# Streamed weight sums and x in the free halves of the weight slots, w_out left where it is, and new byte addresses for g

## The chip, the core and the metric

The kernel runs on one NeuronCore of a Trainium2 chip. The metric is the device time of one execution, in microseconds. The core's engines take their instructions in order, each from its own queue, and meet at semaphores: TensorE (PE; its weight loads are listed as PEld), VectorE (DVE), ScalarE (ACT), GpSimd (POOL), and SyncE (SP), which here issues every DMA.

## The reference, cut to what matters

```python
def _attn_ref(q, k, v):                      # [8, 8, 576, 64], in chunks of 64 rows
    scores = scale * np.matmul(q_c, k_c.transpose(0, 1, 2, 4, 3))
    scores = scores - np.max(scores, axis=-1, keepdims=True)
    attn = np.exp(scores)
    attn = attn / (np.sum(attn, axis=-1, keepdims=True) + 1e-09)
    return np.matmul(attn, v_c)
def _moe_ref(x, w_in, w_out):                # x [4608, 512] is the attention's output
    h = x @ w_in                             # w_in [512, 2048]
    g = h * (1.0 / (1.0 + np.exp(-1.702 * h)))
    return (g @ w_out).astype(np.float32)    # w_out [2048, 512]
```

w_in and w_out come as float64, the rest as float32.

## The kernel before, in words

**Numbers as two words.** Every large product takes its operands as a high and a low float32r word, and one product is three matmuls: high times low, high times high, low times high (L1018 to L1020 and L624 to L626 for h, L1054 to L1056 for the second product, called o below).

**Tiles and batches.** The 4608 tokens are 36 tiles of 128, in 9 batches n of 4 tiles (512 tokens). The 2048 hidden units are 16 blocks j of 128, and g = 16 n + j counts blocks over the whole run. For each block PE makes h in one PSUM bank (`hp`, two buffers), ACT applies the gate and writes `g_h`, DVE writes `g_l`, and PE adds the block's share to four accumulating banks `po` (one for each token tile, 12 matmuls of 512 columns for a block, stationary side `g_h` or `g_l`, moving side the words of w_out). After 16 blocks ACT or DVE copies `po` to `ob` (two buffers) and a DMA stores it.

**Batches 0 and 1** make h directly: 12 matmuls of 512 columns for each block, stationary the words of w_in, moving x. **Batches 2 to 8** make h for two blocks at a time (a pair p, 8 of them) by a seven-product scheme for 2 x 2 blocks: 7 products of 6 matmuls of 256 columns in four phases (`phase`, L624 to L626), whose results DVE and ACT put together (L629, L634). Its stationary operands are three blocks of w_in as they are and four sums of blocks; its moving operands are seven forms of x.

**Slots.** Sixteen slots `w0` to `w15` of 8 KB in each partition hold a block's weights after they are read and split: the first half of a slot, `wt[j][:, 0]`, the words of w_in, the second half, `wt[j][:, 1]`, those of w_out. Before its weights arrive a slot serves the attention of the first tiles.

**The preparation** (`plan_prep`, for each pair) runs while batches 0 and 1 compute. POOL forms the sums (L505 to L515), ACT and DVE split them into words in a tile of their own, `split` (L525 to L533, in slot 0 or 1 by turns from pair 1 on), and DMAs write it all to a scratch tensor `seven` in DRAM: the three plain blocks (`out_a`, L538) and the sums (`out_s`, L548). The words of w_out are written to a second scratch tensor, `second` (`out_o`, L542), and read back pair by pair into slots 8 to 15 (`in_o`, L553), because slots 1 to 6 turn into x of the even batches (`xo`) and into the ring.

**The ring.** In batches 2 to 8 the operands of every pair are read from `seven` again, in four loads (L614; 256 KB, then three of 512 KB) into a ring of six places of 4 KB for each partition: two in each of slots 5 and 6, one in slot 4, one in the second half of `xe3`. A place is free once its phase has run. x of the odd batches lies in `xe0` to `xe3`.

**The attention** of token tiles u and u + 1 (a pair of tiles) runs between the blocks: DMAs bring q and k rows (`raw`, L733 and L722, 32 or 64 small DMAs), DVE transposes them (L776), PE makes the scores s of this pair and x of the pair before in one step (L792, L866), then DVE, ACT and POOL make the softmax and DVE transposes it (L841). From batch 2 on ACT stages x in `xa` and `xb` (L900), POOL forms differences (L470) and ACT and DVE write the words (L473, L476).

**What sets the order.** All steps are given to `Plan` with an engine, a cost, a rank and the events that they need; `Plan.emit` plays them through on its own clock, and the order that comes out is the order in each engine's queue. The first steps follow a list, `ORDER`. A DMA's cost there is the time that it holds SP's queue, plus a fixed `HANDOVER`. `LEAD` is how many blocks ahead of its pair a ring load gets its rank.

**Addresses.** Tiles lie one behind the other in each partition. `gelu`, a tile of 32 bytes that only serves to load a table, stands in the middle of them. Slots 0, 1, 3 and 8 to 15 and `xe0` to `xe3` lie ahead of it and start at 128 modulo 512 bytes. Slots 2, 4, 5, 6 and 7 (so the ring), and `g_h` and `g_l` lie behind it and start at 160 modulo 512. All offsets within these tiles that a matmul uses are multiples of 512 bytes.

## Time and profile before

| | |
|---|---|
| median of 3 runs | 868.02 us (866.17 to 869.13) |
| the profiled execution | 871.12 us, span of the core 869.3 us |
| PE busy / weight loads busy | 839.4 us (97%) / 732.8 us |
| DVE / ACT / POOL busy | 550.1 / 380.6 / 123.2 us |
| DMA traffic | 189.91 MB; mean 218 GB/s |
| granted clock of TensorE, mean | 0.99 |

A span runs from the first to the last instruction. Matmuls are pipelined, and their listed durations overlap (one of 512 columns is listed with about 0.40 us though the next starts 0.23 us later); what a matmul costs is read from one start to the next. A row of the timeline gives start, duration, engine, source line, operation, the tiles written and read, shapes and, in brackets, how long the engine had been idle and which instruction ended that. Batch 0 runs to about 136 us, batch 1 from 130 to 243 us, and batches 2 to 8 from 229 us to the end.

### The profile page before, as it was taken

The numbers are of one execution on the slowest core, as the hardware profiler recorded it, in microseconds if no ns is written. First come the engines' busy times: TensorE is split into PE (matmuls) and PEld (weight loads), VectorE is DVE, ScalarE is ACT, GpSimd is POOL, SyncE is SP. The second block draws the span as 40 slices with busy tenths as digits, with TensorE's granted clock in tenths as the row PEclk, the third lists the DMA queues.
The fourth block names the chain that finished last, engine by engine and source line by source line (L and its number), as shares of the span: only waits on it lengthen the run. The fifth ranks groups of instructions, "written<-read, shape, count | busy, mean of one in ns | idle before, by whom it ended". The sixth has DMA issues, their size and how long they took to land.

```text
span 869.3 us, 17292 instructions
## 1 busy us (share of the span) xinstructions
PE 839.4 (97%) x6902; PEld 732.8 (84%) x6902; DVE 550.1 (63%) x788; ACT 380.6 (44%) x556; POOL 123.2 (14%) x102
## 2 busy tenths in 40 slices
PE   7999989799899988999999999999999999999998
PEld 6788877688788877888988888988888989889886
DVE  5788865562665757675867586758675866634333
ACT  5999725352435234344534353435343534423222
POOL 1000163930300020002100020003000300200000
PEclk9999989899999999999999999999999999999999
DMA  9996877995796779888877788888966676557551
GB/s 228 327 292 185 255 223 213 358 344 140 237 281 210 203 215 265 233 228 202 229 211 210 202 213 248 202 209 233 261 173 178 183 222 180 169 170 219 174 165 49
DMA packets 241216, 189.91 MB, mean 218 GB/s; under 512 B 187248, under 2 KB 201584, under 8 KB 239216
## 3 DMA queue, kind: packets, MB, share of 16 engines
q1 hardware_dynamic: 241136, 188.80, 76.6%
q8 instruction: 55, 0.90, 0.4%
q14 instruction: 25, 0.20, 0.1%
HBM read 156.24 MB, written 32.51 MB: 217 GB/s over the span
## 4 chain that ended last, share of the span: by engine, by line
PE 78%; DMA 11%; SPq 7%; ACT 2%; DVE 1%; issue 1%; DVEq 0%; ACTq 0%
PE po L1054 13%; PE po L1056 13%; PE po L1055 13%; PE hp L625 9%; PE hp L626 9%; PE hp L624 9%; DMA ring<-seven 4%; SPq L733 3%; PE hp L1018 3%; PE hp L1020 2%; PE hp L1019 2%; DMA out_dram<-ob 2%; PE s L792 2%; PE x L866 1%; SPq L297 1%
## 5 line engine op out<-in xcount | busy, mean ns | idle before, releaser
L1054 PE MATMUL po<-second,g_l 128*128 128x512 f32 x448 | 179.1, 400 | 2.3 <-DVE ob L1065 1.8
L1055 PE MATMUL po<-second,g_h 128*128 128x512 f32 x448 | 177.0, 395 | 0.0
L1056 PE MATMUL po<-second,g_h 128*128 128x512 f32 x448 | 176.9, 395 | 0.0
L629 DVE TENSOR_TENSOR d<-hp,d 128x512 f32<-128x512 f32 x168 | 85.5, 509 | 134.1 <-PE hp L626 131.4
L656 ACT ACTIVATE d<-d 128x512 f32<-128x512 f32 x56 | 35.4, 632 | 289.5 <-DVE d L629 289.4
L1056 PEld LDWEIGHTS po<-second,g_h 128*128 128x128 f32 x448 | 84.2, 188 | 20.4
L1054 PEld LDWEIGHTS po<-second,g_l 128*128 128x128 f32 x448 | 84.3, 188 | 18.3 <-DVE ob L1065 2.4
L1055 PEld LDWEIGHTS po<-second,g_h 128*128 128x128 f32 x448 | 84.3, 188 | 14.3
L624 PE MATMUL hp<-xo,ring 128*128 128x256 f32 x320 | 90.1, 281 | 2.6 <-DVE g_l L1045 1.7
L625 PE MATMUL hp<-xo,ring 128*128 128x256 f32 x320 | 90.2, 282 | 0.0
L626 PE MATMUL hp<-xo,ring 128*128 128x256 f32 x320 | 90.1, 281 | 0.0
L822 POOL TENSOR_TENSOR e<-e,r 128x1024 f32<-128x1024 f32 x16 | 32.8, 2051 | 392.8 <-DVE r L819 362.0
L841 DVE STREAM_TRANSPOSE eT<-e 32x512 f32<-32x512 f32 x120 | 84.2, 702 | 5.6 <-POOL e L822 3.8
L624 PE MATMUL hp<-xe,ring 128*128 128x256 f32 x272 | 76.4, 281 | 2.2 <-issue 2.2
L626 PE MATMUL hp<-xe,ring 128*128 128x256 f32 x272 | 76.5, 281 | 0.0
L625 PE MATMUL hp<-xe,ring 128*128 128x256 f32 x272 | 76.5, 281 | 0.0
L661 DVE TENSOR_TENSOR g_l<-f,g_h 128x512 fp32r<-128x512 f32 x56 | 44.7, 799 | 35.5 <-ACT g_h L657 35.4
L624 PEld LDWEIGHTS hp<-xo,ring 128*128 128x128 f32 x320 | 60.4, 189 | 6.4 <-DVE g_l L1045 1.9
L625 PEld LDWEIGHTS hp<-xo,ring 128*128 128x128 f32 x320 | 60.4, 189 | 3.0
L626 PEld LDWEIGHTS hp<-xo,ring 128*128 128x128 f32 x320 | 60.6, 189 | 0.0
L624 PEld LDWEIGHTS hp<-xe,ring 128*128 128x128 f32 x272 | 51.2, 188 | 5.0 <-issue 2.8
L1054 PE MATMUL po<-w,g_l 128*128 128x512 f32 x128 | 52.2, 408 | 2.4 <-ACT ob L1063 2.0
(145 smaller groups left out, 1709.3 us busy)
## 6 DMA issues: line engine op xcount, KB each, us to landing
ring<-seven SPq DMA_DIRECT2D x131, 512.0 KB, 4.5
xe<-seven SPq DMA_DIRECT2D x37, 512.0 KB, 4.5
ring<-seven SPq DMA_DIRECT2D x56, 256.0 KB, 3.2
raw<-in_moe_w_in_dram SPq DMA_DIRECT2D x16, 512.0 KB, 7.6
raw<-in_moe_w_out_dram SPq DMA_DIRECT2D x16, 512.0 KB, 7.6
second<-w SPq DMA_DIRECT2D x16, 512.0 KB, 5.2
out_dram<-ob SPq DMA_DIRECT2D x32, 256.0 KB, 3.2
second<-second SPq DMA_DIRECT2D x8, 1024.0 KB, 8.1
```

The costliest lines, as they stand in the source:

```text
L624: nc.tensor.matmul(hp[:, o], w[:, 0, c], xl[:, c], start=c == 0, stop=False)
L625: nc.tensor.matmul(hp[:, o], w[:, 0, c], xh[:, c], start=False, stop=False)
L626: nc.tensor.matmul(hp[:, o], w[:, 1, c], xh[:, c], start=False, stop=c == 1)
L629: add = lambda out, a, b: nc.vector.tensor_tensor(out, a, b, op=ALU.add)
L656: nc.scalar.activation(t, t, AF.Gelu_apprx_sigmoid)
L661: nc.vector.tensor_tensor(gl, words(h), gh.bitcast(F32), op=ALU.subtract)
L733: nc.sync.dma_start(t[p0 : p0 + 32, i, n, o // 32 : (o + c) // 32, :], src[b, 2 * n + h, s : s + c, d * 32 : d * 32 + 32].rearrange("(t j) ...
L822: nc.gpsimd.tensor_tensor(st["e"], st["e"], bc(st["r"]), op=ALU.mult)
L841: nc.vector.transpose(st["et"][po : po + 32, :, 32 * a : 32 * a + 32], st["e"][pi : pi + 32, :, 32 * b : 32 * b + 32],)
L1054: nc.tensor.matmul(po, gl[:, c], w[:, 0, :], start=j == 0, stop=False)
L1055: nc.tensor.matmul(po, gh[:, c], w[:, 0, :], start=False, stop=False)
L1056: nc.tensor.matmul(po, gh[:, c], w[:, 1, :], start=False, stop=j == NF - 1)
```

## The change

The words of w_out stay in the second halves of their slots for the whole run; `second`, `out_o` and `in_o` are gone. Two exceptions are moved once, by a DMA within SBUF: those of slot 0 to the first half of slot 1 and those of slot 7 to the first half of slot 2, because slots 0 and 7 are used as whole tiles later (`xb`, `raw`). The first halves take what had slots of its own: x of the even batches in slots 3, 4, 5, 6, 8, 9 and 10, and the ring in slots 11 to 15; the sixth place stays in `xe3`. The sums of a pair are split into the first halves of the pair's own two slots, over the words of w_in, so a pair's split needs both h of batch 1 on that pair and the three plain blocks written out; then two DMAs of 512 KB write it to `seven`. Ring places are handed out first come, first served. `Plan` gets a fourth resource, `bus`: a bulk DMA holds SP for 0.5 us and then one shared bus for its cost. `LEAD` goes from 8 to 12 and `EARLY` (the rank of the attention steps) from 4 to 3. `gelu` is 512 bytes instead of 32, which puts all slots, `g_h` and `g_l` at 128 modulo 512.

```diff
+
+    def bulk(self, cost, rank, fn, need=(), make=None, take=(), give=()):
+
+        self.add(DMA, 0.5, rank, fn, need=need, make=make + "~", take=take)
+        self.add(BUS, cost, rank, None, need=[make + "~"], make=make, give=give)
...
-    EARLY = 4
+    EARLY = 3
     K_ACT = (1, 2, 3, 4)
-    LEAD = 8
-    PREP = 4
-    PREP_FROM = 15
+    LEAD = 12
...
     seven = dram.tile([NF // 2, P, 7 * 512], F32, tag="seven", name="seven")
-    second = dram.tile([NF // 2, P, 2 * 1024], F32, tag="second", name="second")
-    X_SLOT, MIXED, RING, SECOND_RAW, W_OUT = (1, 2, 3), 4, (5, 6), 7, 8
     PLAIN = 2
+    STAGE, SECOND_RAW = 0, 7
+    MOVED = {STAGE: 1, SECOND_RAW: 2}
+    X_SLOT, RING = (3, 4, 5, 6, 8, 9, 10), (11, 12, 13, 14, 15)
...
     def x_part_of(n, i, hl):
 
-        if i < 6:
-            return held["x", n % 2, i // 2][:, hl, i % 2]
-        return held["x", n % 2, 3][:, 0, hl]
+        if n % 2:
+            return held["x", i // 2][:, hl, i % 2] if i < 6 else held["x", 3][:, 0, hl]
+        return wt[X_SLOT[2 * (i // 2) + hl]][:, 0, i % 2] if i < 6 else wt[X_SLOT[6]][:, 0, hl]
 
     def x_tile(k):
-        held["x", 1, k] = const.tile([P, 2, 2, 512], F32R, tag=f"xe{k}", name=f"xe{k}")
-        if k == 3:
-            held["r", NRING - 1] = held["x", 1, 3][:, 1].rearrange("p w f -> p (w f)")
+        held["x", k] = const.tile([P, 2, 2, 512], F32R, tag=f"xe{k}", name=f"xe{k}")
...
         for i, k, hneed in ((0, 2, st_a), (2, 2, [e("t1")]), (4, 2, [e("t2")]), (6, 1, [e("t4")])):
             if n == PLAIN:
-                hneed = hneed + [f"al_{X_SLOT[i // 2] if i < 6 else MIXED}"]
+                hneed = hneed + [f"po_{X_SLOT[min(i + 1, 6)] // 2}"]
             if n == PLAIN + 1:
                 hneed = hneed + [f"xal_{i // 2}"]
             plan.add(ACT, 0.55 * k, rank, lambda i=i, k=k: hi(i, k), need=hneed, make=e(f"h{i}"))
...
-        tags = ("stage", "wtmp") if p == 0 else (f"w{(p - 1) % 2}",)
-
-        def hi():
...
+        def half(i):
+            return wt[2 * p + i][:, 0].rearrange("p a b -> p (a b)").rearrange("p (s w f) -> p s w f", s=2, w=2)
+
+        def hi(i):
+            nc.scalar.activation(half(i)[:, :, 0], st["s"][:, 2 * i : 2 * i + 2], AF.Copy)
+
+        def lo(i):
+            w = half(i)
+            nc.vector.tensor_tensor(
+                w[:, :, 1], st["s"][:, 2 * i : 2 * i + 2], w[:, :, 0].bitcast(F32), op=ALU.subtract
+            )
 
-        def out_o(u):
-            w = wt[2 * p + u][:, 1].rearrange("p w f -> p (w f)").bitcast(F32)
-            nc.sync.dma_start(second[p, :, 1024 * u : 1024 * u + 1024], w)
...
-        def in_o():
-            held["o", p] = t = const.tile([P, 2, 2, 512], F32R, tag=f"w{W_OUT + p}", name=f"second_{p}")
-            nc.sync.dma_start(t.rearrange("p u w f -> p (u w f)").bitcast(F32), second[p])
-
-        rank, late = PREP + 2 * p, 11 + p
+        def out_s(i):
+            at = 1024 + 1024 * i
+            w = wt[2 * p + i][:, 0].rearrange("p a b -> p (a b)").bitcast(F32)
+            nc.sync.dma_start(seven[p, :, at : at + 1024], w)
+
+        first = (PLAIN - 1) * NF + 2 * p
+        rank = first - 2
         e = lambda a: f"{a}_{p}"
         w0, w1 = f"w_{j0}", f"w_{j1}"
-        plan.add(POOL, 1.05, rank, lambda: whole(0), need=[w0, f"w_{PREP_FROM}"], make=e("pa0"), take=["tmp"])
+        outs = [e(f"pout{i}") for i in range(3)]
+        for i in range(3):
+            plan.bulk(0.75, first - 6, lambda i=i: out_a(i), need=[w0 if i < 2 else w1], make=outs[i])
+        plan.add(POOL, 1.05, rank, lambda: whole(0), need=[w0, f"w_{NF - 1}"], make=e("pa0"), take=["tmp"])
         plan.add(POOL, 1.05, rank, lambda: whole(1), need=[w1, e("pa0")], make=e("pa"))
         plan.add(POOL, 2.4, rank, sums, need=[e("pa")], make=e("psum"), take=["tmp"], give=["tmp"])
-        plan.add(ACT, 1.08, rank, hi, need=[e("psum")], make=e("phi"), take=[("tmp" if t == "wtmp" else t) for t in tags])
-        plan.add(DVE, 1.25, rank, lo, need=[e("phi")], make=e("plo"), give=["tmp"])
-        outs = []
-        for i in range(3):
-            outs.append(e(f"pout{i}"))
-            plan.add(DMA, 0.6, late, lambda i=i: out_a(i), need=[w0 if i < 2 else w1], make=outs[-1])
         for i in range(2):
-            outs.append(e(f"oout{i}"))
-            plan.add(DMA, 0.6, late, lambda i=i: out_o(i), need=[w0, w1][i : i + 1], make=outs[-1])
-        outs.append(e("pouts"))
-        plan.add(DMA, 1.4, rank, out_s, need=[e("plo")], make=e("pouts"), give=[("tmp" if t == "wtmp" else t) for t in tags])
-        plan.add(None, 0, rank, None, need=outs, make=e("po"))
-        plan.add(DMA, 1.4, PLAIN * NF + 2 * p - 4, in_o, need=[e("po")], make=e("second"), take=[f"w{W_OUT + p}"])
+            plan.add(
+                ACT, 0.6, rank, lambda i=i: hi(i), need=[e("psum"), f"h_{first + 1}", e("pa")] + outs, make=e(f"phi{i}"),
+            )
+            plan.add(
+                DVE, 0.69, rank, lambda i=i: lo(i), need=[e(f"phi{i}")] + [e("plo0")] * i, make=e(f"plo{i}"),
+                give=["tmp"] * i,
+            )
+            plan.bulk(1.44, rank, lambda i=i: out_s(i), need=[e(f"plo{i}")], make=e(f"pouts{i}"))
+        plan.add(None, 0, rank, None, need=[e("pouts0"), e("pouts1")], make=e("po"))
...
     def plan_slots():
-        def ring(k):
-            t = const.tile([P, 2, 1024], F32R, tag=f"w{(MIXED, *RING)[k]}", name=f"ring_{k}")
-            if k:
-                held["r", 2 * k - 1] = t[:, 0]
-            else:
-                held["x", 0, 3] = t[:, :1].rearrange("p o (w f) -> p o w f", w=2)
-            held["r", 2 * k] = t[:, 1]
-
...
-        for j in range(NF):
-            done = [f"o_{(PLAIN - 1) * NF + j}_{t}" for t in range(TB)] + [f"po_{j // 2}"]
-            plan.add(None, 0, -1000, None, need=done, give=[f"w{j}"])
-            if j in X_SLOT:
-                plan.add(None, 0, -1000, lambda j=j: odd(j - 1), need=done + ["prepped"], make=f"al_{j}", take=[f"w{j}"])
-            elif MIXED <= j < SECOND_RAW:
-                plan.add(None, 0, -1000, lambda j=j: ring(j - MIXED), need=done, make=f"al_{j}", take=[f"w{j}"])
+        def move(a, b):
+            nc.sync.dma_start(wt[b][:, 0].bitcast(F32), wt[a][:, 1].bitcast(F32))
+
+        for a, b in MOVED.items():
+            g = (PLAIN - 1) * NF + a
+            plan.bulk(1.44, g, lambda a=a, b=b: move(a, b), need=[f"po_{b // 2}"], make=f"moved_{a}")
+            done = [f"o_{g}_{t}" for t in range(TB)] + [f"po_{a // 2}", f"moved_{a}"]
+            plan.add(None, 0, -1000, None, need=done, give=[f"w{a}"])
         for k in range(4):
             need = [f"h_{(PLAIN - (k < 2)) * NF - 1}"]
             plan.add(None, 0, -1000, lambda k=k: x_tile(k), need=need, make=f"xal_{k}")
-        plan.add(None, 0, -1000, None, need=[f"po_{p}" for p in range(NF // 2)], make="prepped")
+        flat = lambda t: t.rearrange("p a b -> p (a b)")
+        for j in RING:
+            plan.add(None, 0, -1000, lambda j=j: ring_free.append(flat(wt[j][:, 0])), need=[f"po_{j // 2}"], give=["ring"])
+        plan.add(None, 0, -1000, lambda: ring_free.append(flat(held["x", 3][:, 1])), need=["xal_3"], give=["ring"])
...
     def plan_seven(n, p):
         g0 = n * NF + 2 * p
-        first = ((n - PLAIN) * (NF // 2) + p) * 4
         st = {}
         e = lambda a: f"{a}_{g0}"
-        slot = lambda i: held["r", (first + i) % NRING]
-
         def load(i):
             a, b = LOADS[i]
-            nc.sync.dma_start(slot(i)[:, : 512 * (b - a)].bitcast(F32), seven[p, :, 512 * a : 512 * b])
+            st["w", i] = ring_free.pop(0)
+            nc.sync.dma_start(st["w", i][:, : 512 * (b - a)].bitcast(F32), seven[p, :, 512 * a : 512 * b])
...
         for i, (a, b) in enumerate(LOADS):
-            q = first + i
-            need = [f"al_{MIXED + (q + 1) // 2}"] if q < NRING - 1 else ["xal_3"] if q < NRING else [phase_of[q - NRING]]
-            phase_of[q] = e(f"ph{i}")
+            plan.bulk(
+                0.72 * (b - a), g0 - LEAD + 0.1 * i, lambda i=i: load(i), need=[f"po_{p}"], make=e(f"ld{i}"), take=["ring"],
+            )
             plan.add(
-                DMA, 0.5 * (b - a), g0 - LEAD, lambda i=i: load(i), need=need + [f"po_{p}"], make=e(f"ld{i}"),
+                None, 0, g0, lambda i=i: ring_free.append(st["w", i]), need=[e(f"ph{i}")], give=["ring"],
             )
...
         def o_pe(t):
             gh, gl = g_t[g]
-            w = held["o", j // 2][:, j % 2] if n >= PLAIN else wt[j][:, 1]
+            w = wt[MOVED[j]][:, 0] if n >= PLAIN and j in MOVED else wt[j][:, 1]
...
-                PE, 0.69, g + 2.5, lambda t=t: o_pe(t), need=[ev("gl") + ("_0" if g < NH and t < 2 else ""), f"second_{j // 2}" if n >= PLAIN else f"w_{j}"]
+                PE, 0.69, g + 2.5, lambda t=t: o_pe(t), need=[ev("gl") + ("_0" if g < NH and t < 2 else ""), f"moved_{j}" if n >= PLAIN and j in MOVED else f"w_{j}"]
...
     def gelu_table():
-        z = const.tile([P, 8], F32, tag="gelu", name="gelu")
+        z = const.tile([P, P], F32, tag="gelu", name="gelu")
```

**SP's queue between batches 0 and 1, before.** `raw_8` and `raw_10` are the q and k rows of the attention at tiles 8 and 10, `v_8` its v, `ob_0_0` and the like the output of batch 0.

```order
L538 DMA seven_80<-w_5_626 128x2x256
L733 DMA raw_8_1093<-in_q_dram 32x8x32 x12
L733 DMA raw_8_1093<-in_k_dram 32x8x32 x16
L542 DMA second_81<-w_4_584 128x1024
L542 DMA second_81<-w_5_626 128x1024
L538 DMA seven_80<-w_6_718 128x2x256 x2
L548 DMA seven_80<-split_0_1292 128x1024
L548 DMA seven_80<-split_0_1293 128x1024
```

The same place of SP's queue with the change:

```order
L538 DMA seven_80<-w_9_862 128x2x256
L714 DMA raw_8_1093<-in_q_dram 32x8x32 x12
L714 DMA raw_8_1093<-in_k_dram 32x8x32 x16
L538 DMA seven_80<-w_10_889 128x2x256 x2
L538 DMA seven_80<-w_11_968 128x2x256
L538 DMA seven_80<-w_12_1048 128x2x256 x2
L538 DMA seven_80<-w_13_1060 128x2x256
L538 DMA seven_80<-w_14_1133 128x2x256 x2
L538 DMA seven_80<-w_15_1198 128x2x256
L714 DMA raw_10_1349<-in_q_dram 32x8x32 x4
```

From the v rows of tile 6 to the last q rows of tile 8, 15 plain blocks are now issued where 9 plain blocks and 4 writes to `second` were; between tile 8's k rows and the first output store, 9 plain blocks and 12 DMAs for tile 10 now stand where 7 plain blocks, 6 writes to `second`, 2 split sums and 4 DMAs for tile 10 did. All 24 plain blocks are out before tile 10's rows.

**ACT's queue around block 22, before.** `split_4`, `_5` and `_6` are the high words of the sums of pairs 4 to 6, `xa_2` is the staging of x.

```order
L1040 ACTIVATE g_h_21_1717<-hp_21_1693 128x512
L525 ACTIVATE split_4_1734<-sums_4_1677 128x4x256
L525 ACTIVATE split_5_1813<-sums_5_1721 128x4x256
L900 ACTIVATE xa_2_1827<-x_8_0_1778 128x2x4x64
L900 ACTIVATE xa_2_1827<-x_8_1_1779 128x2x4x64
L525 ACTIVATE split_6_1858<-sums_6_1819 128x4x256
```

The same place of ACT's queue with the change:

```order
L1021 ACTIVATE g_h_21_1693<-hp_21_1674 128x512
L527 ACTIVATE w_4_583<-sums_2_1540 128x2x256
L527 ACTIVATE w_5_625<-sums_2_1540 128x2x256
L881 ACTIVATE xa_2_1791<-x_8_0_1744 128x2x4x64
L881 ACTIVATE xa_2_1791<-x_8_1_1745 128x2x4x64
```

Ahead of the staging now stands the split of pair 2 in two pieces instead of those of pairs 4 and 5; pair 4's split follows h of block 25.

**SP's queue ahead of batch 2, before.** `ring_0` to `ring_2` are slots 4 to 6; the first four loads are those of pair 0.

```order
L614 DMA ring_0_1886<-seven_80 128x512
L548 DMA seven_80<-split_7_1894 128x2048
L614 DMA ring_1_1928<-seven_80 128x1024 x2
L614 DMA ring_2_1973<-seven_80 128x1024
L614 DMA ring_2_1973<-seven_80 128x512
L733 DMA raw_12_2009<-in_q_dram 32x8x32 x16
```

With the change, where `w_11` to `w_13` on the left are ring places and `seven_80<-w_12` and `<-w_13` the split sums of pair 6:

```order
L595 DMA w_11_968<-seven_80 128x512
L543 DMA seven_80<-w_12_1048 128x1024
L543 DMA seven_80<-w_13_1060 128x1024
L714 DMA raw_14_2152<-in_q_dram 32x8x32 x4
L595 DMA w_12_1048<-seven_80 128x1024
L595 DMA w_13_1060<-seven_80 128x1024
L714 DMA raw_14_2152<-in_q_dram 32x8x32 x4
L303 DMA v_12_2259<-in_v_dram 128x8x64
L714 DMA raw_14_2152<-in_q_dram 32x8x32 x8
L595 DMA xe3_2291<-seven_80 128x1024
```

The first load now stands behind tile 12's rows and the others behind the writes of pair 6, two of them into its slots. Before, all four were ahead of tile 12's rows.

More of the change, by code (lines that the diff above doesn't have):

```diff
@@ L17 @@
 AX = mybir.AxisListType
-PE, ACT, DVE, POOL, DMA = "pe", "act", "dve", "pool", "dma"
+PE, ACT, DVE, POOL, DMA, BUS = "pe", "act", "dve", "pool", "dma", "bus"
 ORDER = {
@@ L48 @@
 class Plan:
-    HANDOVER = {None: 0.0, PE: 0.25, ACT: 0.12, DVE: 0.12, POOL: 0.15, DMA: 2.9}
+    HANDOVER = {None: 0.0, PE: 0.25, ACT: 0.12, DVE: 0.12, POOL: 0.15, DMA: 2.9, BUS: 2.4}
     TABLE_LOAD = 1.3
@@ L123, in emit @@
                     for i in users.get(ev, ()):
-                        if (self.steps[i][0] == engine and engine != DMA) != same:
+                        to = self.steps[i][0]
+                        if (to == BUS or (to == engine and engine != DMA)) != same:
                             continue
@@ L186, in tile_chunk_attention_ffn @@
     buffers.update({f"po{t}": 1 for t in range(TB)})
[L187 removed]
+    buffers.update(tmp=NTMP, g=3, raw=1, v=1, tr=1, e=1, et=1, stage=1, ring=0)
     plan = Plan(buffers)
@@ L989, in plan_pair @@
             plan.add(
-                ACT, 0.6, rank + 1.5, lambda c=c: x_stage(c), need=[done] + [f"xs_{u}"] * c + ["prepped"] * (u % TB // 2), make=f"xs_{u + c}",
+                ACT, 0.6, rank + 1.5, lambda c=c: x_stage(c), need=[done] + [f"xs_{u}"] * c , make=f"xs_{u + c}",
                 take=[] if c else ["stage" if u % TB == 0 else "w0"], give=["att" if pe else "hp"],
```

35 lines of the change are left out of this document (7 added, 28 removed).

## The prediction

> **What bounds the kernel now.** I read the page first (the span, the busy shares, the groups), then the list of waits of TensorE, then the timeline around its longest waits with the granted clock there, and last SP's queue.
>
> ```profile
> span 869.3 us, 17292 instructions
> PE 839.4 (97%) x6902; PEld 732.8 (84%) x6902; DVE 550.1 (63%) x788; ACT 380.6 (44%) x556; POOL 123.2 (14%) x102
> L1054 PE MATMUL po<-second,g_l 128*128 128x512 f32 x448 | 179.1, 400 | 2.3 <-DVE ob L1065 1.8
> L624 PE MATMUL hp<-xo,ring 128*128 128x256 f32 x320 | 90.1, 281 | 2.6 <-DVE g_l L1045 1.7
> L624 PE MATMUL hp<-xe,ring 128*128 128x256 f32 x272 | 76.4, 281 | 2.2 <-issue 2.2
> ```
>
> PE is the bound: 839.4 of 869.3 us, so 29.9 us are idle. The number of matmuls is the same with the change. The time can therefore fall in only two ways: PE's idle time (and the half clock that follows a long one) shrinks, or one matmul gets shorter. The change touches both.
>
> **A. The address of g.** A listed duration overlaps the next matmul, so I read from start to start. Here are first rows of groups of 12 matmuls: three of 512 columns in batch 1, then two groups of 256 columns in batch 3.
>
> ```profile
> 191.19 0.39 PE L1054 MATMUL po<-w,g_l 128*128 128x512 f32 x1
> 193.94 0.39 PE L1018 MATMUL hp<-x_l,w 128*128 128x512 f32 x1
> 196.69 0.39 PE L1054 MATMUL po<-w,g_l 128*128 128x512 f32 x1
> 199.49 0.39 PE L1018 MATMUL hp<-x_l,w 128*128 128x512 f32 x1
> ...
> 270.46 0.40 PE L1054 MATMUL po<-second,g_l 128*128 128x512 f32 x1
> 273.27 0.28 PE L624 MATMUL hp<-xo,ring 128*128 128x256 f32 x1
> ...
> 400.31 0.28 PE L624 MATMUL hp<-xe,ring 128*128 128x256 f32 x1
> 401.73 0.28 PE L624 MATMUL hp<-xe,xe 128*128 128x256 f32 x1
> 403.17 0.40 PE L1054 MATMUL po<-second,g_l 128*128 128x512 f32 x1
> ```
>
> The group from 191.19 is o of block 23 out of slot 7: moving w_out at 160 modulo 512, stationary g at 160. It takes 193.94 - 191.19 = 2.75 us, 229.2 ns for one. The group from 193.94 is h of block 26 out of slot 10, both sides at 128: 196.69 - 193.94 = 2.75 too. The group from 196.69 is o of block 24 out of slot 8: moving at 128, stationary at 160. It takes 199.49 - 196.69 = 2.80, 233.3 ns. The group from 270.46, out of `second` (slots 8 to 15, so 128 against 160), takes 2.81, 234.2 ns. So a matmul of 512 columns costs 4.2 to 5.0 ns more where its two sides differ modulo 512; I take 4.6. This is an association in one trace, over groups that also differ in slot and neighbour.
>
> How many are affected after tile 8's scores: 448 of L1054, and as many of L1055 and L1056, make 1344; in batch 1 o out of slots 0, 1, 3 and 8 to 15 is 11 x 12 = 132, and h out of slots 2 and 4 to 7, against x at 128, is 5 x 12 = 60. Together 1536 x 4.6 ns = 7.1 us. What is gained ahead of tile 8's scores is lost in that wait.
>
> With 256 columns the sign is not the same: the group at 400.31 (ring at 160, `xe` at 128) takes 1.42 us, 118.3 ns, and the one at 401.73 (both at 128) 1.44 us, 120.0 ns. About 1365 matmuls of 256 columns change from unlike to like: 3 x 272 with `xe`, and of the 3 x 320 with `xo` the four sevenths whose form of x lies in slots 1 and 3, 549. At 0 to 1.7 ns they cost 0 to 2.3 us; I take 1.0. A is **-6.1**, with bounds 0 and -8.
>
> The Trainium skill, "TensorE: Matmul & The Clock Gate", section "Step-by-step: what each phase is for", says that PE has two independent read ports in SBUF and that loading the next weights takes no read bandwidth from the running matmul. By that rule A would be nothing. The trace's 229 and 233 ns differ where only the addresses, slot and neighbour do, so here it does not bear the rule out, and a rival below keeps it.
>
> **B. The wait for tile 8's scores.**
>
> ```profile
> 89.95 1.63 SPq L538 DMA_DIRECT2D seven<-w  x3
> 91.63 1.33 SPq L542 DMA_DIRECT2D second<-w  x2
> ...
> 94.29 3.09 SPq L538 DMA_DIRECT2D seven<-w  x3
> ...
> 104.41 6.41 SPq L733 DMA_DIRECT2D raw<-in_q_dram  x12
> ...
> 120.41 1.25 DVE L776 STREAM_TRANSPOSE qkT<-raw 128x1024 f32<-128x1024 f32 x1 [2.59 <-DMA raw<-in_k_dram]
> 121.80 1.99 PE L792 MATMUL s<-qkT 64*64 64x64 f32 x64 [3.13 <-DVE qkT L776]
> ...
> 120.87:127.70 6.83, 5.90 (x133) 5.35 (x134) 4.12 (x6) 1.09 (x2) 1.44 (x2) 0.50 1.02 379
> ```
>
> PE waits 3.13 us for the transpose, and that for the k rows. The last row is a window: its length, the busy time of PE, its weight loads, DVE, ACT and POOL, the granted clock, the DMA share and GB/s. At clock 0.50, half of PE's 5.90 us, 2.95, is lost in addition. Between 89.95 and 104.41 SP issues 9 plain blocks (256 KB) and 4 writes to `second` (512 KB); with the change 15 plain blocks. By bytes that is 3.84 MB for 4.35, and 12% of 14.46 us would be 1.7 us earlier at most. By the time on SP a plain block takes 1.63/3 = 0.54 to 3.09/3 = 1.03 us and a write to `second` 1.33/2 = 0.67, so six more of the one and four fewer of the other make it 0.6 to 3.5 later. The rows show SP busy without a break here, so I go between the two answers: **+0.8**, and the half clock stays.
>
> **C. The first output store.**
>
> ```profile
> 130.24 0.60 ACT L1063 ACTIVATE ob<-po 128x512 f32<-128x512 f32 x1 [3.62 <-PE po L1056]
> 136.66 0.41 SPq L1070 DMA_DIRECT2D out_dram<-ob  x1
> 145.34 0.60 ACT L1063 ACTIVATE ob<-po 128x512 f32<-128x512 f32 x1 [3.52 <-DMA out_dram<-ob]
> 145.99 0.50 PE L1054 MATMUL po<-w,g_l 128*128 128x512 f32 x1 [1.96 <-ACT ob L1063]
> ```
>
> The copy is done at 130.84, its store is issued 5.8 us later behind the writes of weights, and the next copy and PE wait for its buffer. With the change 6 writes to `second` and 2 split sums no longer stand ahead of it (8 x 512 KB); 2 plain blocks and 8 more of the small DMAs for tile 10 do. A store 2 us earlier removes the wait; I take **-1.5** (bounds 0 and -1.96).
>
> **D. The staging of x behind a split.**
>
> ```profile
> 169.55 1.06 ACT L525 ACTIVATE split<-sums 128x1024 fp32r<-128x1024 f32 x1 [4.09 <-DMA seven<-split]
> 170.51 1.07 ACT L900 ACTIVATE xa<-x 128x512 f32<-128x512 f32 x2
> 171.15 0.80 PE L1018 MATMUL hp<-x_l,w 128*128 128x512 f32 x1 [5.27 <-ACT xa L900]
> 168.65:175.48 6.83, 4.33 (x10) 3.46 (x11) 3.58 (x3) 2.03 (x3) 6.67 (x7) 0.50 1.02 386
> ...
> seven<-split SPq DMA_DIRECT2D x7, 1024.0 KB, 6.3
> seven<-split SPq DMA_DIRECT2D x2, 512.0 KB, 5.7
> ```
>
> ACT stood 4.09 us in front of a split that needs its `split` buffer, which the DMA of the pair before (6.3 us) had not left. Behind it stood the staging of x, which frees the bank that PE's next h needs: 5.27 us idle, then 4.33/2 = 2.2 us at half clock. With the change a split goes into its own pair's slots: no buffer is handed on, its plain blocks were written out long before, and pair 2's sums are formed by POOL before block 22. What can still delay it is POOL, busy 6.67 of those 6.83 us; I leave 1 us of the 7.5. **-6.5** (bounds 0 and -7.5). If POOL is late instead, all of it comes back.
>
> **E. Into batch 2.**
>
> ```profile
> 213.27 0.39 PE L1054 MATMUL po<-w,g_l 128*128 128x512 f32 x1
> 229.35 0.28 PE L624 MATMUL hp<-xo,ring 128*128 128x256 f32 x1
> 233.92 0.39 PE L624 MATMUL hp<-xo,ring 128*128 128x256 f32 x1 [0.89 <-ACT d L634]
> 237.35 0.39 PE L624 MATMUL hp<-xo,ring 128*128 128x256 f32 x1 [1.68 <-DVE g_l L1045]
> ...
> ring<-seven SPq DMA_DIRECT2D x131, 512.0 KB, 4.5
> ```
>
> The two waits, 0.89 and 1.68, are for ACT and DVE. In the new order the exponentials of tile 12 come behind h of block 31 and their transposes on DVE later, so about half goes: **-1.35** (bounds +1.5 and -2.57). New here is the chain of the ring: pair 6's split needs h of block 29, which ends at 213.27. Two pieces on ACT and DVE (half of the 1.06 of D on each engine and piece, about 2 us in all), a write (5.7) and the ring load into the same slot (4.5) make 12.2: 225.5. Batch 2 starts at 229.35 and its second phase, the first to use these places, some 2 us later, so about 5 us are spare. The loads also stand behind four DMAs of tile 14, which wait for `raw`. This hides the chain as long as the split is no more than that late.
>
> **F, G. Waits in batches 2 to 4.**
>
> ```profile
> 311.92 1.25 DVE L776 STREAM_TRANSPOSE qkT<-raw 128x1024 f32<-128x1024 f32 x1 [4.41 <-DMA raw<-in_k_dram]
> 313.21 0.50 PE L792 MATMUL s<-qkT 64*64 64x64 f32 x17 [2.40 <-DVE qkT L776]
> ...
> 337.52 0.35 PE L624 MATMUL hp<-xe,ring 128*128 128x256 f32 x1 [0.64 <-issue]
> 340.02 0.36 PE L624 MATMUL hp<-xe,ring 128*128 128x256 f32 x1 [1.56 <-issue]
> ```
>
> Tile 16's scores wait 2.40 us for k rows. With the change its last k rows stand two ring loads earlier in SP's queue, and the loads of `second` for pairs 5 to 7 are gone from ahead of them; two loads at the 0.4 us that SP takes for one leave little, but 3 MB less does the rest: **-1.7** (bounds +1 and -2.4). The next two waits sum to 2.20 and are at ring operands; with loads ranked 12 blocks ahead, not 8, I take **-1.3** (bounds 0 and -2.2).
>
> The two moves within SBUF (one slot half each) lie beside batch 1; o of block 0 of batch 2 is the first to need them, and I put them at nothing. If the cover is gone it is one write, 5.7 us.
>
> **The sum.** -6.1 + 0.8 - 1.5 - 6.5 - 1.35 - 1.7 - 1.3 = -17.65, so a span of 851.65. The median of the runs (868.02) stands 1.28 under the span of the profiled execution (869.3, itself 871.12 as a run), so **850.4 us**.
>
> **Rivals.**
> 1. *The address does nothing.* The 4.6 ns come from the slot or the neighbour. Against it: two places of batches 1 and 2 agree within 1 ns. The rest stays: 850.4 + 6.1 = 856.5. This is also what the Trainium skill's rule on the two read ports in A would have.
> 2. *The stalls stay.* DMA and SP, not the slots, set B, D, F and G: the DMA share is 1.02 in both windows at half clock, which speaks for it, and 379 and 386 GB/s are far over the mean. Then only A, B and C move: -6.8, 861.2.
> 3. *Slower: a late ring.* If pair 6's split comes more than about 5 us late (POOL behind, or SP held by tile 14's rows), PE stands before pairs 0 and 2 of batch 2, each for a write and a load, 5.7 + 4.5 = 10.2, and each followed by 6.83/2 = 3.4 at half clock: 27.2 over 850.4 is 877.6. Against it are the 5 us spare; for it that this chain is new and no row shows it.
> 4. *Better.* B's wait goes too, by bytes: 850.4 - 0.8 - 3.13 - 2.95 = 843.5, and with all lower bounds of C to G about 840.
>
> **How the numbers follow.** The forecast has a chance of 0.55, rival 1 0.12, rival 2 0.20, rival 3 0.08, rival 4 0.05. A measurement of this kernel tells about 0.3%, 2.6 us, from no change. Faster takes the forecast, rivals 1 and 4 and nearly all of rival 2, 0.87 with a little cut for mishaps; within 0.3% is 0.05, from rival 2 and a half late ring; slower is rival 3, 0.08. The likeliest case's own range is 844 to 857, from A's bounds and D's; to hold 8 in 10 the range reaches to rivals 1, 2 and 4: 840 to 863.
>
> **What would show it.** A: groups of 12 matmuls of o in 2.75 us throughout, not 2.81. B: tile 8's scores behind a wait of 3 to 4 us, clock 0.50 behind it. C and D: no wait of PE over 1 us between 140 and 200, no second window of clock 0.50 there. E: the first phases of batch 2 not waiting for DMA. The forecast is wrong if PE's idle time after the change is still near 30 us or the groups stay at 2.81.

## The result and the profile after

| | before | with the change |
|---|---|---|
| median | 868.58 us (866.17 to 869.89, 4 runs) | 856.0 us (854.67 to 856.94, 4 runs) |
| ratio to before | 1 | 0.9857 (95%: 0.983 to 0.9884) |
| span of the profiled execution | 869.3 us | 855.2 us |
| PE busy / idle | 839.4 / 29.9 us | 831.5 / 23.7 us |
| DMA traffic | 189.91 MB | 174.18 MB |

The time falls by 12.4 us by the ratio; the forecast was 17.6 (850.4 us, range 840 to 863). The spans of the two profiled executions differ by 14.1. One of the six executions of kernel 7 below took 1645.5 us, in a slow state, and is left out of its row. From the page of the changed kernel, with the groups that answer to those of before:

```profile
span 855.2 us, 17331 instructions
PE 831.5 (97%) x6902; PEld 732.5 (86%) x6902; DVE 545.5 (64%) x795; ACT 380.8 (45%) x563; POOL 121.6 (14%) x102
L1035 PE MATMUL po<-w,g_l 128*128 128x512 f32 x576 | 229.0, 398 | 3.0 <-DVE ob L1046 1.6
```

As many matmuls, 7.9 us less of busy PE, 6.2 us less of idle PE. PE's waits with the change (engine, line, what it waited for: us in all, times, the longest):

```profile
PE hp L605 <- issue: 2.5, 2, 1.9
...
PE s L773 <- DVE qkT L757: 2.5, 1, 2.5
PE hp L605 <- DMA w<-seven: 2.4, 1, 2.4
```

The wait of 5.3 us for `xa` is gone. That for tile 8's scores has become shorter, that for tile 16's scores is gone. In their place stand waits in front of the phases of h: for a ring load (DMA `w<-seven`), for DVE, and the two marked "issue". Row by row:

```profile
119.61 0.30 PE L773 MATMUL s<-qkT 64*64 64x64 f32 x5 [2.47 <-DVE qkT L757]
141.28 0.50 PE L1035 MATMUL po<-w,g_l 128*128 128x512 f32 x1 [0.79 <-DVE ob L1046]
220.04 0.38 PE L605 MATMUL hp<-w,w 128*128 128x256 f32 x1 [1.14 <-ACT d L615]
234.03 0.35 PE L605 MATMUL hp<-w,w 128*128 128x256 f32 x1 [2.44 <-DMA w<-seven]
308.71 0.39 PE L605 MATMUL hp<-w,xe 128*128 128x256 f32 x1 [1.60 <-DVE d L610]
325.53 0.35 PE L605 MATMUL hp<-xe,w 128*128 128x256 f32 x1 [1.87 <-issue]
```

The window of half clock behind the first of them (length, busy time of PE, its weight loads, DVE, ACT and POOL, granted clock, DMA share, GB/s):

```profile
120.60:124.02 3.42, 3.42 (x81) 3.01 (x72) 2.06 (x3) 1.09 (x2) 0.00 (x0) 0.50 0.98 324
```

There is this one window of half clock where there were two of 6.83; a window of 3.41 us at 28 us and one of under 3 us at the end stand in both traces. What a window costs I take as the time of its matmuls from start to start less that of as many of their kind at full clock: 2.5 and 2.05 us before, 1.6 now.

### The profile page after: what moved, and what is told of

It reads as the page before. It is cut to its first block, busy times and chain, and to the rows that moved or that the text cites. A ratio compares the mean times of both kernels' runs of the same rounds, so it can differ in the third digit from the quotient of the medians.

```text
span 855.2 us, 17331 instructions
## 1 busy us (share of the span) xinstructions
PE 831.5 (97%) x6902; PEld 732.5 (86%) x6902; DVE 545.5 (64%) x795; ACT 380.8 (45%) x563; POOL 121.6 (14%) x102
## 2 busy tenths in 40 slices
DMA packets 239056, 174.18 MB, mean 204 GB/s; under 512 B 187008, under 2 KB 201344, under 8 KB 238976
## 4 chain that ended last, share of the span: by engine, by line
PE 80%; SPq 7%; DMA 6%; DVE 3%; ACT 2%; issue 2%; POOL 0%; DVEq 0%; POOLq 0%; ACTq 0%
PE po L1035 13%; PE po L1036 13%; PE po L1037 13%; PE hp L605 10%; PE hp L607 10%; PE hp L606 10%; SPq L714 5%; PE hp L999 2%; PE hp L1001 2%; PE hp L1000 2%; PE s L773 2%; PE x L847 2%; DMA raw<-in_k_dram 1%; DMA xe<-seven 1%; SPq L303 1%
## 5 line engine op out<-in xcount | busy, mean ns | idle before, releaser
L1035 PE MATMUL po<-w,g_l 128*128 128x512 f32 x576 | 229.0, 398 | 3.0 <-DVE ob L1046 1.6
L1036 PE MATMUL po<-w,g_h 128*128 128x512 f32 x576 | 226.4, 393 | 0.0
L1037 PE MATMUL po<-w,g_h 128*128 128x512 f32 x576 | 225.0, 391 | 0.0
L1035 PEld LDWEIGHTS po<-w,g_l 128*128 128x128 f32 x576 | 108.9, 189 | 24.7 <-DVE ob L1046 2.6
L1037 PEld LDWEIGHTS po<-w,g_h 128*128 128x128 f32 x576 | 108.6, 189 | 23.7
L1036 PEld LDWEIGHTS po<-w,g_h 128*128 128x128 f32 x576 | 109.0, 189 | 17.6
L605 PE MATMUL hp<-w,w 128*128 128x256 f32 x360 | 102.0, 283 | 4.4 <-DMA w<-seven 2.4
L607 PE MATMUL hp<-w,w 128*128 128x256 f32 x360 | 101.8, 283 | 0.0
L606 PE MATMUL hp<-w,w 128*128 128x256 f32 x360 | 101.8, 283 | 0.0
L605 PE MATMUL hp<-xe,w 128*128 128x256 f32 x272 | 76.9, 283 | 2.6 <-issue 2.5
L607 PE MATMUL hp<-xe,w 128*128 128x256 f32 x272 | 77.0, 283 | 0.0
L606 PE MATMUL hp<-xe,w 128*128 128x256 f32 x272 | 76.9, 283 | 0.0
L605 PEld LDWEIGHTS hp<-w,w 128*128 128x128 f32 x360 | 68.8, 191 | 8.1 <-issue 2.8
L606 PEld LDWEIGHTS hp<-w,w 128*128 128x128 f32 x360 | 68.8, 191 | 2.4
L607 PEld LDWEIGHTS hp<-w,w 128*128 128x128 f32 x360 | 68.8, 191 | 0.0
L642 DVE TENSOR_TENSOR g_l<-f,g_h 128x512 fp32r<-128x512 f32 x56 | 39.8, 710 | 35.3 <-ACT g_h L638 35.1
L757 DVE STREAM_TRANSPOSE qkT<-raw 128x1024 f32<-128x1024 f32 x30 | 37.2, 1242 | 33.7 <-DMA raw<-in_k_dram 16.1
L605 PEld LDWEIGHTS hp<-xe,w 128*128 128x128 f32 x272 | 52.0, 191 | 5.4 <-issue 3.3
```

The source lines that it names most:

```text
L605: nc.tensor.matmul(hp[:, o], w[:, 0, c], xl[:, c], start=c == 0, stop=False)
L606: nc.tensor.matmul(hp[:, o], w[:, 0, c], xh[:, c], start=False, stop=False)
L607: nc.tensor.matmul(hp[:, o], w[:, 1, c], xh[:, c], start=False, stop=c == 1)
L642: nc.vector.tensor_tensor(gl, words(h), gh.bitcast(F32), op=ALU.subtract)
L757: nc.vector.transpose(st["tr"][:, i].rearrange("p n (t j) -> p (n t) j", j=32), st["raw"][:, i].rearrange("p n t j -> p (n t) j"),)
L1035: nc.tensor.matmul(po, gl[:, c], w[:, 0, :], start=j == 0, stop=False)
```

## The experiments

The first two columns give the median beside that of the kernel before on the same chip, the third the ratio with its 95% interval; three kernels ran once each.

| kernel | us | before | ratio |
|---|---|---|---|
| 1. changed, `gelu` 32 bytes | 862.56 | 867.52 | 0.994 (0.9914 to 0.9966) |
| 2. before, `gelu` 512 bytes | 861.65 | 867.52 | 0.9926 (0.9898 to 0.9953) |
| 3, 4, 5. changed, `gelu` 256, 64, 128 bytes | 859.77, 861.01, 853.23 | | one execution each |
| 6. before, pair 5's split behind the staging | 870.29 | 867.11 | 1.0045 (1.002 to 1.0071) |
| 7. changed, w_out written to DRAM again | 862.92 | 867.11 | 0.9952 (0.9931 to 0.9972) |
| 8. changed, tile 14's k rows behind ring loads | 855.23 | 867.11 | 0.9861 (0.9839 to 0.9882) |
| 9. changed, `EARLY` 4 | 857.13 | 867.11 | 0.9895 (0.9875 to 0.9915) |
| 10. the changed kernel again | 857.13 | 867.42 | 0.989 (0.9856 to 0.9923) |
| 11. changed, plain blocks behind tile 8's k rows | 851.73 | 867.42 | 0.9822 (0.979 to 0.9854) |
| 12. 8 and 11 together | 850.24 | 867.42 | 0.9805 (0.9776 to 0.9834) |

### The address alone, undone and done (1, 2)

```diff
-        z = const.tile([P, P], F32, tag="gelu", name="gelu")
+        z = const.tile([P, 8], F32, tag="gelu", name="gelu")
```

> The changed kernel with gelu at 32 bytes again, so that g and slots 2, 4, 5, 6 and 7 start at 160 modulo 512, and slots 0, 1, 3 and 8 to 15 and xe0 to xe3 at 128; the order of all engines is the same. Theory A (a 512-column matmul is longer where its two sides differ modulo 512): o out of 11 of 16 blocks is unlike, 924 matmuls in batches 2 to 8 and 132 in batch 1, and 60 of h, 1116 x 4.3 ns = +4.8 us; about 512 matmuls of 256 columns become unlike, 512 x 1.2 ns = -0.6; together +4.2, 860.2 us. Rival (the address does nothing, the groups differed by slot or neighbour): 856.0 within 0.5.

In the kernel before, the same line the other way round:

> The kernel before with gelu at 512 bytes, so that g, all slots and the ring are at 128 modulo 512; the order of all engines is the same. Theory A: 1536 matmuls of 512 columns lose 4.3 ns, -6.6 us, about 1365 of 256 columns gain 1.2 ns, +1.6; -5.0, so about 863.5 us, with PE's waits unchanged within 1 us in all. Rival (the address does nothing): 868.5 within 1.

Both came out on the side of theory A. Undone, the changed kernel is 0.994 of the kernel before, where the change has 0.9857; its 862.56 us lie above the 860.2 expected, and its profiled execution has two more windows of 3.41 us at half clock than that of the change. Done alone, it is 0.9926, 6.4 us by its ratio (4.1 to 8.8), where 5.0 was expected: about half of the whole gain comes from one line. The traces say it without the spread of the runs. Means from one start to the next, over all neighbouring matmuls of one width without a wait: in the kernel before 232.4 ns for 512 columns and 118.6 for 256; with `gelu` at 512 bytes 228.7 and 119.6, and in the changed kernel 228.6 and 119.6. With the address alone PE still waits 3.3 us at the first store, 3.0 for tile 8's scores and 2.8 for `xa` in the profiled execution. Its idle time there is 24.6 us for 29.9, not within 1 us as expected, so the ratio holds some change of the waits beside the pace.

### Which distance counts (3, 4, 5)

Here `gelu` has 256, 64 and 128 bytes ([P, 64], [P, 16], [P, 32]).

> The changed kernel with gelu at 256 bytes: g and slots 2, 4, 5, 6 and 7 start at 384 modulo 512, the others at 128. Theory that the two sides must be alike modulo 512: groups of 12 matmuls of o out of slots 8 to 15 in 2.80 us, as at 32 bytes, about 860 us. Rival, that a shorter period (256 or less) decides: 2.75 us everywhere, 856 us.

> The changed kernel with gelu at 64 bytes: g and slots 2, 4, 5, 6 and 7 start at 192 modulo 512, the others at 128. Theory that the two sides must be alike modulo 512: o out of slots 8 to 15 in 2.80 us for 12, about 860 us. Rival, that alike modulo 64 is enough: 2.75 us everywhere, 856 us.

> The changed kernel with gelu at 128 bytes: g and slots 2, 4, 5, 6 and 7 start at 256 modulo 512, the others at 128. A distance of 256 cost nothing, distances of 32 and 64 did. If the period is 128: 229 ns between starts in both kinds of groups; if it is 256: 233 ns for o out of slots 8 to 15, 1056 x 4.3 ns = 4.5 us more.

Block 24 out of slot 8, first matmul of o and first of the h that follows, 12 matmuls later. In this order: the changed kernel (distance 0 between w_out and g), 32 bytes (distance 32), 64 bytes (64), 128 bytes (128) and 256 bytes (256):

```profile
183.78 0.39 PE L1035 MATMUL po<-w,g_l 128*128 128x512 f32 x1
186.50 0.39 PE L999 MATMUL hp<-x_l,w 128*128 128x512 f32 x1
```

```profile
187.66 0.39 PE L1035 MATMUL po<-w,g_l 128*128 128x512 f32 x1
190.45 0.39 PE L999 MATMUL hp<-x_l,w 128*128 128x512 f32 x1
```

```profile
184.11 0.40 PE L1035 MATMUL po<-w,g_l 128*128 128x512 f32 x1
186.91 0.39 PE L999 MATMUL hp<-x_l,w 128*128 128x512 f32 x1
```

```profile
180.80 0.40 PE L1035 MATMUL po<-w,g_l 128*128 128x512 f32 x1
183.59 0.40 PE L999 MATMUL hp<-x_l,w 128*128 128x512 f32 x1
```

```profile
183.94 0.39 PE L1035 MATMUL po<-w,g_l 128*128 128x512 f32 x1
186.66 0.39 PE L999 MATMUL hp<-x_l,w 128*128 128x512 f32 x1
```

2.72, 2.79, 2.80, 2.79 and 2.72 us. Over all o of the traces with the two sides that far apart, some 1050 matmuls each and 1670 at distance 0: 228.9, 232.7, 233.4, 231.9 and 229.1 ns. So by these five distances what counts is the distance modulo 256, not 512: of my two expectations that went by 512 the one for 64 bytes came true, and the one for 256 did not. The same instructions in the same slot and the same order change their pace with the address alone, which takes away the rival of the slot and the neighbour. The times of these single executions do not follow their pace. At 128 bytes the wait for tile 8's scores is 0.30 us and that at batch 2's ring load 0.34, with the same order: SP came to the plain blocks ahead of tile 8's rows at 86.84 us, 1.7 sooner than in the changed kernel. Such waits come and go between executions by 1 to 2 us of DMA.

### Whose fault the staging's wait was (6)

```diff
-        plan.add(ACT, 1.08, rank, hi, need=[e("psum")], make=e("phi"), ...
+        plan.add(ACT, 1.08, rank, hi, need=[e("psum")] + ["xs_9"] * (p >= 5), make=e("phi"), ...
```

> The kernel before, with the split of pair 5 placed behind the staging of x in ACT's queue (pair 4's stays ahead of it). Theory D (ACT stands before a split whose buffer is still being written out, and the staging behind it holds PE): PE's wait of 5.27 us at 171 falls under 1.5 us and the half clock there goes; -4 to -7 us, 861 to 864. Rival (the staging or PE waits for the traffic of that stretch whatever the order): the wait stays over 4 us, 867 to 868.

Neither came out whole. The wait at 171 is gone, as the theory had it, but the kernel is slower by 0.45%. ACT's rows, and the two new waits of PE:

```profile
166.56 1.09 ACT L900 ACTIVATE xa<-x 128x512 f32<-128x512 f32 x2 [2.05 <-PE x L866]
167.87 1.06 ACT L525 ACTIVATE split<-sums 128x1024 fp32r<-128x1024 f32 x1 [0.23 <-POOL whole L505]
176.95 1.06 ACT L525 ACTIVATE split<-sums 128x1024 fp32r<-128x1024 f32 x1 [8.01 <-DMA seven<-split]
182.69 1.06 ACT L525 ACTIVATE split<-sums 128x1024 fp32r<-128x1024 f32 x1 [1.19 <-DMA seven<-split]
...
180.37 0.50 PE L1018 MATMUL hp<-x_l,w 128*128 128x512 f32 x1 [2.52 <-DVE g_l L1045]
188.48 0.50 PE L1018 MATMUL hp<-x_l,w 128*128 128x512 f32 x1 [2.32 <-DVE g_l L1045]
```

The staging runs at once now, and ACT stands 8.01 us at pair 6's split instead, with g of the next blocks behind it. The place of the staging only chose who pays. The stall is that of splits which hand on two buffers, each held by its write.

### Bytes on the DMA, with the splits in their own slots (7)

Here 16 DMAs of 512 KB write the words of w_out to DRAM again; nothing reads them.

```diff
...
+        for i in range(2):
+            plan.bulk(1.44, first - 6, lambda i=i: out_o(i), need=[w0, w1][i : i + 1], make=e(f"oout{i}"))
```

> The changed kernel with the words of w_out written to a scratch tensor in DRAM again (16 DMAs of 512 KB that nothing reads). Ahead of tile 8's k rows SP then issues 9 plain blocks and 6 such writes, 15 DMAs as without them, but 5.4 MB for 3.9 MB. Theory that the bytes set when these rows arrive: 1.5 MB at the 0.32 to 0.38 MB/us of the windows there is 4 to 5 us later, tile 8's scores wait 6 to 7.5 us for 2.47, with two windows of half clock, and the first store is late again: +6 to +10, 862 to 866. Rival that the number of DMAs on SP sets it: the wait stays 2.5 us, 856 to 857.5. By both, the wait of PE at the staging of x does not come back, since a split waits for no other pair's write.

```profile
110.62 7.84 SPq L721 DMA_DIRECT2D raw<-in_k_dram  x16
121.86 0.39 PE L780 MATMUL s<-qkT 64*64 64x64 f32 x4 [6.31 <-DVE qkT L764]
145.80 0.79 PE L1042 MATMUL po<-w,g_l 128*128 128x512 f32 x1 [3.34 <-DVE ob L1053]
165.12 1.09 ACT L888 ACTIVATE xa<-x 128x512 f32<-128x512 f32 x2 [2.51 <-PE x L854]
```

862.92 us, in the range of the theory of the bytes. The waits at tile 8's scores (6.31) and at the first output (3.34) come back with the writes, and the half clock beside each. The k rows are issued 2.06 us later than with the change (110.62 for 108.56) and the scores start 2.25 later, half of the 4 to 5 that I worked out, so the 6.31 meets the expected 6 to 7.5 in part by luck: the rest of the longer wait is PE, which comes to it 1.6 us sooner after as many matmuls, mostly since this execution has no window of half clock at 28 us (about 1.5). The 15 DMAs ahead of the rows hold SP for 12.0 us here and for 9.8 with the change, which is the 2.06; from the end of issuing to the transpose it is 2.0 us for 1.8. ACT goes from the split to the staging without standing before a buffer, and no wait of PE over 0.25 us lies between 146 and 225, with the DMAs as full as before the change (from 165 to 175 us share 1.02 and 365 GB/s, before 1.02 and 386). So the writes, by the time that they hold SP, made B and C; D stays away with the traffic back.

### The ring at batch 2, and EARLY (8, 9)

SP's queue in the changed kernel, behind the waits above: the load of 228.08 goes into a place whose phase had run by 223.7, and PE waits for it until 234.03.

```profile
222.08 0.94 SPq L595 DMA_DIRECT2D w<-seven  x1
223.12 0.85 SPq L543 DMA_DIRECT2D seven<-w  x2
224.36 3.62 SPq L714 DMA_DIRECT2D raw<-in_k_dram  x4
228.08 0.40 SPq L595 DMA_DIRECT2D w<-seven  x1
228.57 0.38 SPq L595 DMA_DIRECT2D xe<-seven  x1
```

```diff
-                        need=raw[:1] if i + n else [f"qk_1_{NP - 1}_{u - 2}"] if u - 2 >= NPE else [], ...
+                        need=(raw[:1] if i + n else [...]) + ["ld3_34~"] * (u == 14 and i * n > 0), ...
```

> The changed kernel with 12 of the 16 k-row DMAs of tile 14 placed behind the last two ring loads of pair 1 of batch 2 in SP's queue. Theory (these loads were late because four row DMAs of 3.62 us stood ahead of them, with their place free since 224): PE's wait of 2.44 us at 234 goes, -1.5 to -2.4, 853.6 to 854.5, if the rows are still in time for tile 14's scores. Rival (the loads' own transfer or the place sets it, or the rows come late in turn): 856 or more.

```profile
224.26 1.81 SPq L595 DMA_DIRECT2D w<-seven  x1
226.16 0.56 SPq L595 DMA_DIRECT2D xe<-seven  x1
...
232.22 0.36 PE L605 MATMUL hp<-w,w 128*128 128x256 f32 x1 [0.45 <-DMA w<-seven]
332.72 0.50 PE L1035 MATMUL po<-w,g_l 128*128 128x512 f32 x1 [2.75 <-DVE ob L1046]
456.08 0.36 PE L605 MATMUL hp<-w,w 128*128 128x256 f32 x1 [2.46 <-DMA w<-seven]
```

The load is issued at 224.26, and the wait falls from 2.44 to 0.45: what was late was SP's queue, four rows of 0.9 us each. But the time is 0.9861, that of the changed kernel (0.9857 and 0.989): waits of 2.75 and 2.46 us stand further on, in an order that is another from here to the end.

> The changed kernel with EARLY at 4, as before the change, so that the steps of the attention rank a block earlier. Theory (the waits of PE at 294 to 336, 5.7 us together, are DVE standing before a transpose whose rows are late): rows a block earlier take 2 to 4 us off, 852 to 854. Rival (rows and ring loads share SP's queue, so the ring loads come late instead): 856 to 858.

The edit is `EARLY = 3` to 4. 0.9895 is the rival's side, but not told apart from the changed kernel. The waits between 294 and 336 do not go; they become one:

```profile
314.69 1.25 DVE L757 STREAM_TRANSPOSE qkT<-raw 128x1024 f32<-128x1024 f32 x1 [5.17 <-DMA w<-seven]
317.07 0.55 PE L605 MATMUL hp<-xe,w 128*128 128x256 f32 x1 [4.96 <-issue]
```

DVE stands 5.17 us before the transpose of rows, and what frees PE's PSUM bank stands behind it. The same pair of rows explains "issue" in the changed kernel: DVE's transpose at 321.85 there had waited 5.69 us for k rows, DVE empties PE's bank until 325.43 (both rows stand under F below), and PE's phase starts at 325.53.

### A shorter queue ahead of tile 8's rows (10, 11, 12)

```diff
-            plan.bulk(0.75, first - 6, lambda i=i: out_a(i), need=[w0 if i < 2 else w1], make=outs[i])
+            plan.bulk(0.75, first - 6, lambda i=i: out_a(i), need=[w0 if i < 2 else w1] + ["qk_1_3_8"] * (p > 2), make=outs[i])
```

> The changed kernel itself once more, beside the two that follow: 0.986 of the kernel before (0.983 to 0.989), 855 to 856 us by all theories. A ratio outside that would say that the comparisons between sessions are not good to 0.3%.

> The changed kernel with the plain blocks of pairs 3 to 7 (15 DMAs of 256 KB) issued only behind tile 8's k rows; 6 of the 15 that stood between these rows and those of tile 6 go behind. Theory (bytes ahead of these rows set the wait at tile 8's scores): 1.5 MB less is 4 us earlier, the wait of 2.47 us falls under 0.5 and no half clock follows it (1.7): -3 to -4.5, 851.5 to 853, about 0.981 of the kernel before. Rival (the rows start when their buffer is free, or the plain blocks come back as a wait at the first store or at a split): within 1 us of the changed kernel.

> The kernel of the run before with tile 14's k rows behind the ring loads of pair 1 as well. If the two waits are independent: -3 to -4.5 for the first and up to -2 for the second, 850 to 852.5. If what is saved at batch 2's start comes back as a later wait, as it did when that edit was made alone: the same as the run before within 1 us.

The changed kernel again gave 0.989, on the edge of the expected interval, and 857.13 us, over the expected 855 to 856; the medians of its two sessions differ by 1.1 us. Beside it, 0.9822 for the plain blocks behind the rows, 5.4 us less by the medians and 3.2 by the spans of the profiled executions (851.5 for 854.7). SP's k rows of tile 8, and the window around its scores:

```profile
105.46 7.84 SPq L714 DMA_DIRECT2D raw<-in_k_dram  x16
...
114.00:120.00 6.00, 6.00 (x147) 4.97 (x145) 4.15 (x5) 1.18 (x2) 5.76 (x7) 1.00 0.60 175
```

PE is busy without a gap at clock 1.00; the wait and its half clock are gone, as the theory had it. At 128 bytes the wait was nearly gone without this edit, so the rows have to show whose work it is: from the first plain block to the last k row SP takes 23.8 us here (89.55 to 113.30), and 27.9, 28.2 and 27.4 in the changed kernel's two traces and at 128 bytes. The rows come 3.1 us earlier than in the changed kernel though SP began 1.0 later, and it is again SP's time that went. With both edits 0.9805, 850.24 us: faster than either kernel of this study, and the changed kernel's interval beside it (0.9856 to 0.9923) does not reach it. The part of the second edit, 0.0017, is within the intervals.

## Why the prediction was right, and where it was not

| term | forecast, us | measured, us |
|---|---|---|
| A address | -6.1 | -7.9 + 2.3 = -5.6 |
| B tile 8's scores | +0.8 | -0.7 (3.13 to 2.47), half clock 2.5 to 1.6: -1.5 |
| C first store | -1.5 | -1.2 (1.96 to 0.79) |
| D staging | -6.5 | -7.3 (5.27 and 2.05 of half clock) |
| E into batch 2 | -1.35 | +1.0 (2.57 to 1.14 + 2.44), two smaller waits of 1.28 gone |
| F tile 16 | -1.7 | 0 (2.40 to 0.79 + 1.60) |
| G ring, batch 3 | -1.3 | +0.3 (2.20 to 1.87 + 0.66) |

The measured side of A is the difference of the means times the number: 3.77 ns x 2088 and 0.98 x 2352. With the two smaller waits all terms come to -15.6 for a span that is 14.1 shorter; the 1.5 us between them I have not placed. That the time lies well inside the range is in part luck: B came 2.3 us better than forecast, and E, F and G 5.7 worse (+1.3 for -4.35).

**A** was right in its mechanism, and experiments 1 to 5 make a cause of what the prediction called an association. Mis-sized was the loss at 256 columns, +2.3 for +1.0: the unlike ones went from 118.4 to 119.6 ns, 1.2 where 1.0 us over 1365 had meant 0.7, and those that were alike before, at 118.9 to 119.1, came to 119.6 too. The rival that the address does nothing falls. The Trainium skill, "TensorE: Matmul & The Clock Gate", section "Step-by-step: what each phase is for", lets the load of the next weights take nothing from the running matmul, by which the addresses should not matter; the 229 and 233 ns of the same matmuls at distance 0 and 64 do not bear that out. Why the distance matters no run shows.

**B** had the wrong sign. SP's queue up to tile 8's rows, with the change:

```profile
88.52 4.22 SPq L538 DMA_DIRECT2D seven<-w  x6
...
93.59 2.10 SPq L538 DMA_DIRECT2D seven<-w  x3
...
98.54 3.49 SPq L538 DMA_DIRECT2D seven<-w  x6
102.08 6.44 SPq L714 DMA_DIRECT2D raw<-in_q_dram  x12
```

The 15 plain blocks held SP for 4.22 + 2.10 + 3.49 = 9.8 us, 0.65 each, where I had up to 1.03, and the stretch is 13.56 us for 14.46. The prediction's two answers were 1.7 us earlier by bytes and 0.6 to 3.5 later by SP; it is 0.9 earlier, and I had gone to the other side. The stretch began 1.4 us sooner too (88.52 for 89.95).

**C and D** came out as forecast. The first output store is issued at 131.18 us for 136.66. On D, experiment 6 shows that the staging's place in the queue was not at fault, and that moving it costs time; experiment 7 excludes the traffic. With their own slots the splits also came to lie further apart on ACT (144.76, 155.64 and 168.77 us for 151.21, 156.90, 164.40 and 169.55), and no run gave the kernel before more buffers alone, so these two are not told apart.

**E, F and G** fell short by those 5.7 us. Rival 2, that the waits are set by the DMAs and SP, was right in F and G, and what it says holds for E too. E's step "about 5 us are spare" looked at pair 6's chain alone, which was in time. The load that came late was one of pair 1, behind rows in SP's queue; experiment 8 shows it. F removed PE's wait and not the late rows: DVE now stands before transposes of rows, 4.69 and 5.69 us, with PE's banks behind:

```profile
306.83 1.25 DVE L757 STREAM_TRANSPOSE qkT<-raw 128x1024 f32<-128x1024 f32 x1 [4.69 <-DMA raw<-in_k_dram]
308.00 0.65 DVE L610 TENSOR_TENSOR d<-hp,d 128x512 f32<-128x512 f32 x1
...
321.85 1.25 DVE L757 STREAM_TRANSPOSE qkT<-raw 128x1024 f32<-128x1024 f32 x1 [5.69 <-DMA raw<-in_k_dram]
...
324.61 0.82 DVE L610 TENSOR_TENSOR d<-hp,d 128x256 f32<-128x256 f32 x2
```

G misread its wait. The prediction took the two waits at 337 to 340 us to be for ring operands; in the kernel before, too, DVE stood before rows, and PE's phases at 337.52 and 340.02 start 0.1 us after DVE has emptied a bank:

```profile
335.40 1.25 DVE L776 STREAM_TRANSPOSE qkT<-raw 128x1024 f32<-128x1024 f32 x1 [3.04 <-DMA raw<-in_q_dram]
336.57 0.84 DVE L629 TENSOR_TENSOR d<-hp,d 128x256 f32<-128x256 f32 x2
...
339.50 0.42 DVE L629 TENSOR_TENSOR f<-hp,f 128x256 f32<-128x256 f32 x1
```

The means, `LEAD`, makes no difference either: with 8 in place of 12 the steps that `Plan` plays through come out in the same order on all engines. This is read from the program, not from a run.

The late ring as a cause of slowness (rival 3) was seen in small, one wait of 2.44 us without half clock; in experiment 10 PE waited 2.45 us for that load, and in 11 2.81, there with half clock.

## What to carry to other kernels

Read matmuls from start to start and sort them by the addresses of their two sides: half of this gain was one tile's size. Where an engine waits in order for a buffer that a DMA hands on, moving what stands behind it only changes who pays; give it a buffer of its own. And a queue of small row DMAs is priced by what stands ahead of it: look which writes can go behind the rows that PE will want first.
